# Units of 256 tokens taken in pairs of 512 from the seventh on, with g kept in the place of w_in, and a new order of the attention work

## The chip, the cores and the metric

One core of a Trainium2 chip. The metric is the device time of one execution in microseconds; the kernel before took 1070.82 us (median of 3 runs, 1069.51 to 1071.07).

## What is computed

Attention by random features over 8 batches, 8 heads, 576 tokens and head size 64, and then a feed-forward block on the 4608 tokens:

```python
h = proj - sq ; h = h - max(h) ; phi = exp(h) / sqrt(m)      # for q and k, m = 128 features
kv = einsum('bhsm,bhsd->bhmd', k_p, v) ; z = sum(k_p, axis=2)
x = einsum('bhsm,bhmd->bhsd', q_p, kv) / (einsum('bhsm,bhm->bhs', q_p, z) + 1e-06)
h = x @ w_in          # [4608, 512] @ [512, 2048]
g = h - tanh(h)
out = g @ w_out       # [4608, 2048] @ [2048, 512]
```

All matmul operands of the feed-forward block are kept as a high and a low part in the type fp32r, and each product is three matmuls: high by high, high by low, low by high.

## The kernel before

The tokens are cut into 18 units of 256 (`TC`). The weights are decoded once into 16 tiles `wt[f]` of 128 partitions, each with two parts (high, low) of 1024 columns: 512 of w_in (four blocks of 128, index `c`) and 512 of w_out. They stay in SBUF.

**First units.** Units 0 and 1 go together: `ffn_h(0, s)` has matmuls of 512 columns (12 for one of the 16 slices `f`), and four output tiles of 128 tokens are kept in four PSUM banks. This pass runs beside the decoding and the first attention work, up to about 187 us.

**Units 2 to 17.** For each unit there are 8 steps. In a step `ffn_h` (line 468) makes two slices of h with 12 matmuls of 256 columns each, into one PSUM bank (two banks, `h0` and `h1`, in turn). ScalarE takes the tanh (472), VectorE subtracts (473), ScalarE casts to the high part `gh` (474), VectorE makes the low part `gl` (475). The products with w_out for the step before, `ffn_out` (lines 486 to 488), are 12 matmuls of 512 columns into the two output banks `po0` and `po1`. So TensorE's order is h of step s, products of step s-1, h of step s+1. `ffn_store` copies the two output tiles by ScalarE (499) into one buffer of tag `o` and stores them (501).

**Attention.** `k_unit` makes for a batch `b` and a pair of heads `c` what the keys contribute, `q_unit` makes a quarter `c` of the x of a unit `ch`. There are four of each: four query quarters per unit, four key quarters per batch of 576 tokens. They are generators, run beside the feed-forward work: each call of `beat()` moves every open generator to its next `yield` and opens those that the table `start` has for this beat. A step has two beats, so a unit has 16; beat 32 is the start of unit 2 and beat 96 that of unit 6. A query quarter has 7 beats: the load (81), the high and low part of q (75, 129, 130), the features (142 to 150) and the normalisation (347 to 356), two beats of nothing, the transposes (363) with their high and low part (386, 387), the products with the keys' result (393, 394), and `x_split` (406, 407), which writes the high and low part of x into one of the two halves of `xh` and `xl`, one for even and one for odd units. If a unit is reached with `xdone[ch]` under 4, the open generators are run on until it is 4.

**Order and queues.** The instructions are put into each engine's queue by a scheduler that follows the order in which the program names them, and takes an instruction earlier where it is ready earlier. Each engine works its queue in order. All loads and stores are issued by SP's queue.

Of the kernel before, what the change touches and what calls it, by code (L numbers as in the profile page):

```python
# [19 lines left out]
P = 128  # L20
# [3 lines left out]
TC = 256  # L24
NCH = NT // TC
E = D + 2
# [5 lines left out]
def favor_attention_ffn(ctx: ExitStack, tc: tile.TileContext, qT, kT, va, vt, omT, w, out):  # L32
# [283 lines left out]
    def q_unit(ch, c):  # L316
# [47 lines left out]
        if native:  # L364
            qf = att("qt", [P, 2, TC], F32, f"qt_{n}")
            nc.scalar.copy(qf.rearrange("p h t -> p (h t)"), pt)
            yield
            pn = ps.tile([P, TC], F32, tag=bank("pt"), name=f"pn_{n}")
            for b, s, e in pieces:
                for h in range(2):  # L370
                    nc.tensor.matmul(pn[:, s:e], kvf[b][c][:, h], qf[:, h, s:e], start=h == 0, stop=h == 1)
            if ch == 2:
                if c < 2:
                    x2[c] = sb.tile([P, TC], F32, tag="xs", name=f"x2_{c}", bufs=2)
                elif c == 2:
                    x2[3] = sb.tile([P, DM], F32, tag="o", name="x2")
                    x2[2], x2[3] = x2[3][:, 0:TC], x2[3][:, TC:]
                nc.scalar.copy(x2[c], pn)
# [18 lines left out]
        nc.scalar.copy(tmp[0:D], pn[D:P, 0])  # L397
        nc.scalar.copy(tmp[D:P], pn[0:D, 1])
        nc.vector.tensor_add(xs[0:D], pn[0:D, 0], tmp[0:D])
        nc.vector.tensor_add(xs[D:P], pn[D:P, 1], tmp[D:P])  # L400
        yield
        x_split(ch, c, xs, nc.vector)
        xdone[ch] = xdone.get(ch, 0) + 1

    def x_split(ch, c, x, engine):
        nc.scalar.copy(xh[:, ch % 2, c], x)
        engine.tensor_sub(xl[:, ch % 2, c], x, xh[:, ch % 2, c].bitcast(F32))  # L407

# [47 lines left out]
    xh, xl = [sb.tile([P, 2, NC, TC], F32R, name=f"x{k}") for k in "hl"]  # L456

    def ffn_h(ch, s):

# [32 lines left out]
    def ffn_store(ch):  # L492
        for t, p in enumerate(pos[ch]):
            if ch == NCH - 1 and t == 1:
                o = sb.tile([P, DM], F32, tag="g", name=f"o_{ch}_{t}")
                nc.vector.tensor_copy(o, p)
            else:
                o = sb.tile([P, DM], F32, tag="o", name=f"o_{ch}_{t}")
                nc.scalar.copy(o, p)
            r = ch * TC + t * P  # L500
            nc.sync.dma_start(out[r : r + P, :], o)

# [5 lines left out]
    xdone = {}  # L508
    x2 = {}
    gens = []  # L510

    def tick(new=(), force=False):
# [39 lines left out]
    while decoded < NF:  # L552
# [34 lines left out]
    start = {}  # L587
    for ch in range(3, NCH):
# [8 lines left out]
    assert min(start) >= t  # L597

    def beat():
        nonlocal t  # L600
        tick(start.pop(t, ()))
        t += 1
# [3 lines left out]
    for c in range(NC):  # L606
        x_split(2, c, x2[c], nc.vector)
    ffn_out(*prev)
    ffn_store(0)
    mode.update(pj=["pj0", "pj1"], pt=["pt"])  # L610
    prev = None
    for ch in range(2, NCH):
        out_tiles(ch)
        for s in range(NS):
            while ch > 2 and xdone.get(ch, 0) < NC:
                tick((), True)
            g = (ch, s, *ffn_h(ch, s))
            beat()
            if prev is not None:
                ffn_out(*prev)  # L620
                if s == 0:
                    ffn_store(ch - 1)
            beat()
            prev = g
    ffn_out(*prev)
    ffn_store(NCH - 1)
    for name in list(pools)[::-1]:
# [36 lines left out]
```

## Time and profile before

| what | before |
|---|---|
| runs, median (lowest, highest) | 1070.82 us (1069.51, 1071.07) |
| the profiled execution, its own time | 1070.01 us |
| its span, first to last instruction | 1068.2 us |
| mean granted clock of TensorE | 0.991 |
| TensorE, VectorE, ScalarE, GpSimd busy | 1044.0, 854.0, 713.2, 323.5 us |

Times in rows count from the first instruction. In a row of groups the name of the line is followed by engine, operation, what is written and read, and the shape; x is the count, then come the busy time in us, the mean duration of one in ns, and the idle time ahead of it with what ended it. PE is TensorE's matmul, PEld its load of weights, DVE is VectorE, ACT ScalarE, POOL GpSimd, SP the engine that issues the transfers. A matmul's duration holds its way through the array, so matmuls that follow one another overlap in their rows; what a matmul costs in a full stretch is read from start to start. PEclk is the granted clock as a share of 2.4 GHz.

### The profile page before, as it was taken

How to read it: one execution, taken by the hardware profiler on the slowest of the kernel's cores; microseconds unless marked ns; L12 is line 12 of the kernel's file. 1: busy time of each engine (PE TensorE's matmuls, PEld its weight loads, DVE VectorE, ACT ScalarE, POOL GpSimd, SP SyncE). 2: the span in 40 equal slices, each digit the busy share in tenths (PEclk: the TensorE clock that was granted, in tenths of full speed). 3: DMA queues.
4: the chain of work that ended last, by engine and by line, in shares of the span. 5: the costliest groups of instructions: out<-in, count | busy, mean ns of one | idle time of the engine just before them, and what ended most of it. 6: DMA issues, size and time to landing. Idle time of an engine off the chain costs nothing. (4 is left out here: it accounts for less than half of the span.)

```text
span 1068.2 us, 20318 instructions
## 1 busy us (share of the span) xinstructions
PE 1044.0 (98%) x6760; PEld 949.3 (89%) x6760; DVE 854.0 (80%) x3030; ACT 713.2 (67%) x1833; POOL 323.5 (30%) x553
## 2 busy tenths in 40 slices
PE   8988999989999999999999999999999999999998
PEld 7767888988999999999999998999999999999997
DVE  6999985898888986788888888898888897666522
ACT  6997655777676765577777766777767775555422
POOL 4634540344333320133333333233333331000000
PEclk8999999998999999999999999999999999999999
DMA  8750401111111110011111111111101110000000
GB/s 266 234 212 12 178 4 48 43 43 38 33 53 33 53 33 31 11 53 33 52 34 52 34 28 53 33 48 29 51 22 52 29 41 11 30 11 26 1 21 20
DMA packets 35529, 55.91 MB, mean 52 GB/s; under 512 B 12256, under 2 KB 21600, under 8 KB 33376
## 3 DMA queue, kind: packets, MB, share of 16 engines
q1 hardware_dynamic: 35344, 54.57, 16.2%
q8 instruction: 54, 0.88, 0.4%
q14 instruction: 51, 0.42, 0.1%
q10 hardware_dynamic: 80, 0.03, 0.0%
HBM read 45.15 MB, written 9.44 MB: 51 GB/s over the span
## 5 line engine op out<-in xcount | busy, mean ns | idle before, releaser
L468 PE MATMUL h<-xh,w 128*128 128x256 f32 (+1 forms) x2176 | 453.3, 292 | 3.8 <-DVE g L473 2.1
L468 PEld LDWEIGHTS h<-xh,w 128*128 128x128 f32 x2176 | 356.7, 191 | 14.1 <-DVE g L473 2.7
L468 PE MATMUL h<-xl,w 128*128 128x256 f32 (+1 forms) x1088 | 317.3, 292 | 0.5 <-DVE xl L407 0.5
L486 PE MATMUL po<-w,gh 128*128 128x512 f32 x544 | 214.2, 394 | 0.0
L468 PEld LDWEIGHTS h<-xl,w 128*128 128x128 f32 x1088 | 207.9, 191 | 6.7 <-DVE xl L407 0.8
L487 PE MATMUL po<-w,gh 128*128 128x512 f32 x544 | 213.7, 393 | 0.0
L488 PE MATMUL po<-w,gl 128*128 128x512 f32 x544 | 209.3, 391 | 0.0
L473 DVE TENSOR_TENSOR g<-h,g 128x512 f32<-128x512 f32 x144 | 98.8, 686 | 66.4 <-ACT g L472 65.3
L472 ACT ACTIVATE g<-h 128x512 f32<-128x512 f32 x144 | 85.1, 591 | 99.2 <-PE h L468 91.9
L474 ACT CAST gh<-g 128x512 fp32r<-128x512 f32 x144 | 89.4, 621 | 84.3 <-DVE g L473 82.7
L475 DVE TENSOR_TENSOR gl<-g,gh 128x512 fp32r<-128x512 f32 x144 | 109.9, 764 | 38.3 <-ACT gh L474 36.5
L488 PEld LDWEIGHTS po<-w,gl 128*128 128x128 f32 x544 | 102.2, 188 | 20.7
L486 PEld LDWEIGHTS po<-w,gh 128*128 128x128 f32 x544 | 102.5, 188 | 16.6
L487 PEld LDWEIGHTS po<-w,gh 128*128 128x128 f32 x544 | 102.5, 188 | 15.2
L347 DVE CUSTOM_DVE_ANT_0 junk<-phi_q,zb 128x128 f32<-128x128 f32 (+1 forms) x320 | 96.5, 303 | 14.7 <-ACT phi_q L150 0.5
L250 POOL TENSOR_TENSOR khl<-phi_ka,khl 128x256 fp32r<-128x256 f32 x48 | 38.0, 795 | 154.2 <-DVE khl L249 129.2
L150 ACT ACTIVATE phi_q<-phi_q,nb_q 128x128 f32<-128x128 f32 x240 | 79.0, 392 | 6.3 <-DVE nb_q L146 6.1
L258 POOL CAST vhl<-v 128x128 fp32r<-128x128 f32 (+1 forms) x144 | 45.7, 319 | 100.9 <-PE pk L266 82.4
L439 POOL TENSOR_SCALAR a<-a 128x1024 f32<-128x1024 f32 x14 | 59.0, 4214 | 54.7 <-ACT a L435 42.1
L387 DVE TENSOR_TENSOR ql<-pt,qh 128x512 fp32r<-128x512 f32 x60 | 41.1, 685 | 26.5 <-ACT qh L386 26.1
L259 DVE TENSOR_TENSOR vhl<-v,vhl 128x128 fp32r<-128x128 f32 (+1 forms) x144 | 45.2, 314 | 16.7 <-POOL vhl L258 13.0
L146 DVE CUSTOM_DVE_ANT_0 phi_q<-pj_q,phi_q 128x128 f32<-128x128 f32 x240 | 55.9, 283 | 1.1 <-ACT phi_q L143 1.0
(151 smaller groups left out, 1952.9 us busy)
## 6 DMA issues: line engine op xcount, KB each, us to landing
raw<-w SPq DMA_DIRECT2D x16, 1024.0 KB, 7.5
kf<-kT SPq DMA_DIRECT2D x32, 288.0 KB, 2.9
qf<-qT SPq DMA_DIRECT2D x72, 128.0 KB, 2.1
out<-o SPq DMA_DIRECT2D x36, 256.0 KB, 2.0
v<-vt SPq DMA_DIRECT2D x24, 288.0 KB, 2.8
v<-va SPq DMA_DIRECT2D x8, 288.0 KB, 5.8
omf<-omT ACTq DMA_DIRECT2D x1, 32.0 KB, 2.1
omf<-omT SPq DMA_DIRECT2D x1, 32.0 KB, 2.4
```

Source lines behind the costliest of these rows:

```text
L146: nc.vector.tensor_tensor_reduce(ph[:, j], pj[:, i, :M], ph[:, j], scale=-SCALE, scalar=3.0e38, op0=ALU.add, op1=ALU.min, accum_out=nb[:, ...
L150: nc.scalar.activation(ph[:, j], ph[:, j], AF.Exp, bias=nb[:, j : j + 1], scale=-1.0)
L347: nc.vector.tensor_tensor_reduce(bank("junk")[r], ph[r, i], kvs[b, c][1][r, h], scale=1.0, scalar=EPS, op0=ALU.mult, op1=ALU.add, accum_ou ...
L439: engine.tensor_scalar(a.bitcast(F32), a.bitcast(F32), 2.0**-15, 122879.9921875, op0=ALU.max, op1=ALU.min)
L468: nc.tensor.matmul(o, w_, x, start=i == 0, stop=i == len(prods) - 1)
L472: nc.scalar.activation(g, p, AF.Tanh)
L473: nc.vector.tensor_sub(g, p, g)
L474: nc.scalar.copy(gh, g)
L475: nc.vector.tensor_sub(gl, g, gh.bitcast(F32))
L486: nc.tensor.matmul(po[t], h, wt[f][:, 0, DM:], start=first, stop=False)
L487: nc.tensor.matmul(po[t], h, wt[f][:, 1, DM:], start=False, stop=False)
L488: nc.tensor.matmul(po[t], l, wt[f][:, 0, DM:], start=False, stop=last)
```

## The change

From unit 6 on the units go in 6 pairs (`NL`) of 512 tokens. A pass over a pair has 16 steps, one per slice `f`. `wide_h` makes h with 12 matmuls of 512 columns, and g as before, but splits it: the first 256 tokens' g goes on to high and low part by ScalarE and VectorE, and its products with w_out (6 matmuls of 512 columns) follow one step later. The other 256 tokens' g goes by GpSimd into the columns of `wt[f]` that held the first half of w_in. After the 16 steps come the two other output tiles, 48 matmuls each, from there.

The half of w_in that is written over comes from DRAM again for the next pass: in unit 2 w_in is stored to DRAM (16 transfers of 512 KB), and from the eleventh step of the first pass on the w_in of a slice six steps ahead is brought to the columns of the second half, two tiles for one slice, in four transfers of 128 KB; `w_in` names the place. This is done for passes 1 to 5.

x no longer goes from `q_unit` to `xh` and `xl`. It goes to a tile `later` with room for two units, and is split ahead of the unit or pass that uses it: for units 3 to 6 as soon as it is there, for unit 7 behind the last h of unit 5, for the later pairs between the two late output tiles, in pieces of 512 columns. A query quarter waits with its last part until the unit two before it has been split.

A pass has 40 beats: 32 in the steps and 4 in each late output tile. The table of starts is new: listed beats for units 3 to 7 and for batches 2, 3 and 4 (28, 51, 84, with 5, 7 and 9 between the quarters), after that a query quarter every five beats (4.5 for the second pair) and a key quarter every eleven. Attention for a pair is made during the pass before it. Buffers: `kvw` 6 for 7, `qf` 1 for 2, no `tmp`; output tiles take buffers of `gl`, `gh` or `g`.

```diff
+C0 = 6
+NL = (NQ - C0) // 2
+NB = 8
...
-        tmp = att("tmp", [P, TC], F32, f"tmp_{n}")
-        xs = sb.tile([P, TC], F32, tag="xs", name=f"xs_{n}", bufs=2)
...
-        yield
-        x_split(ch, c, xs, nc.vector)
+        while ch > 3 and ch - 2 not in split:
+            yield
+        xs = later[:, c, ch % 2 * TC : ch % 2 * TC + TC]
+        nc.scalar.copy(xs[0:D], pn[D:P, 0])
+        nc.scalar.copy(xs[D:P], pn[0:D, 1])
+        nc.vector.tensor_add(xs[0:D], pn[0:D, 0], xs[0:D])
+        nc.vector.tensor_add(xs[D:P], pn[D:P, 1], xs[D:P])
         xdone[ch] = xdone.get(ch, 0) + 1
...
+    def store(p, r, engine=nc.scalar):
+        o = sb.tile([P, DM], F32, tag=bank("o"), name=f"o_{r}", bufs=1 if mode["o"][-1] == "g" else 2)
+        copy(engine, o, p)
+        nc.sync.dma_start(out[r : r + P, :], o)
+    def w_in_away(f):
+        w_dram[f] = tc.dram_tile([P, 2, DM], F32, name=f"w_in{f}")
+        nc.sync.dma_start(w_dram[f], wt[f][:, :, 0:DM].bitcast(F32))
+    def w_in_back(i):
+        f, k = i % NF, 2 * (i % NB)
+        for j in range(2):
+            for a in range(2):
+                nc.sync.dma_start(wt[k + j][:, a, TC:DM].bitcast(F32), w_dram[f][:, a, TC * j : TC * j + TC])
+    def w_in(a, f, i, c):
+        if a == 0:
+            return wt[f][:, i, c * P : (c + 1) * P]
+        j = TC + c % 2 * P
+        return wt[2 * (f % NB) + c // 2][:, i, j : j + P]
+    def wide_h(a, f):
+        p = ps.tile([P, 2, TC], F32, tag=bank("h"), name=f"h_w{a}_{f}")
+        prods = [(w_in(a, f, i, c), x[:, 0:2, c]) for c in range(NC)
+                 for i, x in ((0, xh), (0, xl), (1, xh))]
+        for i, (w_, x) in enumerate(prods):
+            nc.tensor.matmul(p, w_, x, start=i == 0, stop=i == len(prods) - 1)
+        g = sb.tile([P, 2, TC], F32, tag=bank("o"), name=f"g_w{a}_{f}", bufs=1 if mode["o"][-1] == "g" else 2)
+        e = sb.tile([P, 2, TC], F32R, tag="gh", name=f"ge_w{a}_{f}", bufs=2)
+        nc.scalar.activation(g, p, AF.Tanh)
+        nc.vector.tensor_sub(g, p, g)
+        nc.scalar.copy(e[:, 0], g[:, 0])
+        nc.vector.tensor_sub(e[:, 1], g[:, 0], e[:, 0].bitcast(F32))
+        hi, lo = [wt[f][:, i, 0:TC] for i in range(2)]
+        nc.gpsimd.tensor_copy(hi, g[:, 1])
+        nc.gpsimd.tensor_sub(lo, g[:, 1], hi.bitcast(F32))
+        return a, f, e[:, 0], e[:, 1]
...
-        phi=(ak, 3), qh=(ak, 1), ql=(ak, 1), tmp=(ak, 1), kf=(ak, 1), kx=(ak, 1), qf=(ak, 2),
+        phi=(ak, 3), qh=(ak, 1), ql=(ak, 1), kf=(ak, 1), kx=(ak, 1), qf=(ak, 1),
...
+    def begins(a):
+        return 16 * C0 + 40 * a
+    for ch in range(3, NQ):
+        a, j = (ch - C0) // 2, (ch - C0) % 2 * NC
         for c in range(NC):
-            k = 28 + 4 * c if ch == 3 else 42 + 4 * c if ch == 4 else 16 * (ch - 1) - 6 + 4 * c
+            if ch < C0 + 2:
+                k = [(28,31,34,37),(43,46,49,52),(40,55,58,64),(61,70,76,82),(67,73,79,85)][ch - 3][c]
+            else:
+                k = begins(a - 1) + (-4 + 9 * (j + c) // 2 if a == 1 else -9 + 5 * (j + c))
             start.setdefault(k, []).append(("q", ch, c))
     for b in range(2, B):
+        a = ((b * S) // TC - C0) // 2
         for c in range(NC):
-            k = 31 + 5 * c if b == 2 else 16 * (need[b] - 1) - 25 + 8 * c
+            k = [28,51,84][b - 2] + [5,7,9][b - 2] * c if b < 2 + len([28,51,84]) else begins(a - 1) + -18 + 11 * c
...
+    for a in range(NL):
+        r = (C0 + 2 * a) * TC
+        out_tiles("w")
+        prev = None
+        for f in range(NF):
+            g = wide_h(a, f)
+            beat()
+            if prev is not None:
+                wide_out(*prev)
+            i = NF * a + f + 6
+            if NF <= i < NF * NL:
+                w_in_back(i)
+            beat()
+            prev = g
+        wide_out(*prev)
+        for i in range(2):
+            store(pos["w"][i], r + i * P)
+        for i in range(2):
+            p = ps.tile([P, DM], F32, tag=bank("h"), name=f"last_{a}_{i}")
+            for f in range(NF):
+                products(p, f, *[wt[f][:, j, i * P : (i + 1) * P] for j in range(2)])
+                if f % 4 == 3:
+                    beat()
+            store(p, r + (2 + i) * P, nc.vector if a == NL - 1 and i == 1 else nc.scalar)
+            if i == 0 and a < NL - 1:
+                next_x(a + 1)
```

`products` are the three matmuls of lines 486 to 488, `wide_out` calls it for the two tiles of the first 256 tokens, and `next_x(a)` runs the attention on until the pair's x is there and then splits it.

## Rows read from the trace of the kernel before

**Rows 1.** The page: the span, busy times of the engines, and GB/s by slice.

```profile
span 1068.2 us, 20318 instructions
...
PE 1044.0 (98%) x6760; PEld 949.3 (89%) x6760; DVE 854.0 (80%) x3030; ACT 713.2 (67%) x1833; POOL 323.5 (30%) x553
...
GB/s 266 234 212 12 178 4 48 43 43 38 33 53 33 53 33 31 11 53 33 52 34 52 34 28 53 33 48 29 51 22 52 29 41 11 30 11 26 1 21 20
```

**Rows 2.** Busy time by stretch: length, engines in order, PEclk, DMA share, GB/s.

```profile
187.00:241.00 54.00, 50.72 (x340) 46.30 (x338) 47.55 (x188) 39.38 (x110) 22.88 (x46) 1.00 0.15 42
241.00:309.00 68.00, 66.21 (x435) 61.04 (x436) 61.38 (x237) 49.72 (x135) 27.35 (x54) 0.93 0.16 45
309.00:421.00 112.00, 112.00 (x769) 103.96 (x768) 92.95 (x364) 76.05 (x204) 31.07 (x60) 1.00 0.12 36
529.00:644.00 115.00, 115.00 (x793) 107.00 (x792) 98.98 (x393) 82.56 (x224) 41.42 (x80) 1.00 0.14 41
926.00:975.00 49.00, 49.00 (x326) 44.99 (x325) 31.57 (x115) 28.20 (x70) 0.00 (x0) 1.00 0.06 20
```

**Rows 3.** The same view, around the start of unit 3.

```profile
220.00:236.00 16.00, 16.00 (x105) 14.51 (x104) 15.49 (x63) 11.88 (x34) 7.95 (x16) 1.00 0.16 46
236.00:246.00 10.00, 5.19 (x25) 3.87 (x23) 8.62 (x33) 7.91 (x24) 3.75 (x12) 0.74 0.19 67
241.00:251.00 10.00, 8.21 (x34) 7.31 (x35) 9.67 (x34) 7.48 (x21) 5.26 (x11) 0.50 0.30 87
```

**Rows 4.** Timeline, TensorE's longest wait after 187 us: start, duration, instruction, idle before.

```profile
239.54 0.50 PE L142 MATMUL pj_kb<-om,kx 128*128 128x256 f32 x2 [2.82 <-DVE nb_km L146]
```

**Rows 5.** The chain that ended last, two steps of unit 17: start, duration, piece.

```profile
1044.92 2.87 PE h L468 x24
...
1050.54 2.87 PE h L468 x24
```

**Rows 6.** Timeline of TensorE, first matmul of two steps of units 0 and 1.

```profile
111.79 0.39 PE L468 MATMUL h<-xh,w 128*128 128x512 f32 x1
...
117.23 0.39 PE L468 MATMUL h<-xh,w 128*128 128x512 f32 x1
```

**Rows 7.** Groups of instructions by line and shape.

```profile
L475 DVE TENSOR_TENSOR gl<-g,gh 128x512 fp32r<-128x512 f32 x144 | 109.9, 764 | 38.3 <-ACT gh L474 36.5
...
L473 DVE TENSOR_TENSOR g<-h,g 128x512 f32<-128x512 f32 x144 | 98.8, 686 | 66.4 <-ACT g L472 65.3
L474 ACT CAST gh<-g 128x512 fp32r<-128x512 f32 x144 | 89.4, 621 | 84.3 <-DVE g L473 82.7
...
L387 DVE TENSOR_TENSOR ql<-pt,qh 128x512 fp32r<-128x512 f32 x60 | 41.1, 685 | 26.5 <-ACT qh L386 26.1
...
L250 POOL TENSOR_TENSOR khl<-phi_ka,khl 128x256 fp32r<-128x256 f32 x48 | 38.0, 795 | 154.2 <-DVE khl L249 129.2 <-PE pj_km L142 13.6 <-PE h L468 7.4
...
L407 DVE TENSOR_TENSOR xl<-xs,xh 128x256 fp32r<-128x256 f32 x60 | 27.1, 452 | 1.9 <-ACT xh L406 1.3
...
L406 ACT CAST xh<-xs 128x256 fp32r<-128x256 f32 x60 | 24.5, 409 | 20.5 <-DVE xs L400 20.2
```

**Rows 8.** Timeline of one loaded step: last h, its g, first products.

```profile
601.05 0.28 PE L468 MATMUL h<-xh,w 128*128 128x256 f32 x1
...
605.08 0.68 DVE L473 TENSOR_TENSOR g<-h,g 128x512 f32<-128x512 f32 x1
...
606.45 0.69 DVE L475 TENSOR_TENSOR gl<-g,gh 128x512 fp32r<-128x512 f32 x1 [0.69 <-ACT gh L474]
...
608.16 0.39 PE L486 MATMUL po<-w,gh 128*128 128x512 f32 x1
```

**Rows 9.** Line 475 by itself: duration min/median/max in ns.

```profile
L475 DVE TENSOR_TENSOR gl<-g,gh x144: 676/693/1525, 92.4 to 1061.1; 128x512 fp32r<-128x512 f32 x144
```

**Rows 10.** Transfers by line: count, KB each, median us from issue to landing.

```profile
qf<-qT SPq DMA_DIRECT2D x72, 128.0 KB, 2.1
```

More of the change, by code (lines that the diff above doesn't have):

```diff
@@ L24 @@
 TC = 256
-NCH = NT // TC
+NQ = NT // TC
+C0 = 6
+NL = (NQ - C0) // 2
+NB = 8
 E = D + 2
@@ L372, in q_unit @@
             if ch == 2:
[L373 to L378, printed above, removed]
+                nc.scalar.copy(later[:, c, 0:TC], pn)
             else:
@@ L394, in q_unit @@
                 nc.tensor.matmul(pn[:, h, s:e], w, ql[:, h, s:e], start=False, stop=True)
-        tmp = att("tmp", [P, TC], F32, f"tmp_{n}")
-        xs = sb.tile([P, TC], F32, tag="xs", name=f"xs_{n}", bufs=2)
[L397 to L400, printed above, removed]
-        yield
-        x_split(ch, c, xs, nc.vector)
+        while ch > 3 and ch - 2 not in split:
[5 more added lines that the diff above has]
+        nc.vector.tensor_add(xs[D:P], pn[D:P, 1], xs[D:P])
         xdone[ch] = xdone.get(ch, 0) + 1
     def x_split(ch, c, x, engine):
-        nc.scalar.copy(xh[:, ch % 2, c], x)
-        engine.tensor_sub(xl[:, ch % 2, c], x, xh[:, ch % 2, c].bitcast(F32))
+        r = ch if isinstance(ch, slice) else ch % 2
+        nc.scalar.copy(xh[:, r, c], x)
+        engine.tensor_sub(xl[:, r, c], x, xh[:, r, c].bitcast(F32))
     wt = {}
@@ L456, in favor_attention_ffn @@
     xh, xl = [sb.tile([P, 2, NC, TC], F32R, name=f"x{k}") for k in "hl"]
+    later = sb.tile([P, NC, 2 * TC], F32, name="later")
     def ffn_h(ch, s):
@@ L493, in ffn_store @@
         for t, p in enumerate(pos[ch]):
[L494 to L501, printed above, removed]
+            store(p, ch * TC + t * P)
+    def store(p, r, engine=nc.scalar):
+        o = sb.tile([P, DM], F32, tag=bank("o"), name=f"o_{r}", bufs=1 if mode["o"][-1] == "g" else 2)
+        copy(engine, o, p)
+        nc.sync.dma_start(out[r : r + P, :], o)
@@ L503, in out_tiles, with products, wide_out @@
+    def products(o, f, h, l):
+        nc.tensor.matmul(o, h, wt[f][:, 0, DM:], start=f == 0, stop=False)
+        nc.tensor.matmul(o, h, wt[f][:, 1, DM:], start=False, stop=False)
+        nc.tensor.matmul(o, l, wt[f][:, 0, DM:], start=False, stop=f == NF - 1)
+    def wide_out(a, f, h, l):
+        for t, p in enumerate(pos["w"]):
+            products(p, f, h[:, t * P : (t + 1) * P], l[:, t * P : (t + 1) * P])
     def out_tiles(ch, tags=("po0", "po1")):
@@ L508, in favor_attention_ffn @@
     xdone = {}
-    x2 = {}
+    split = {2}
     gens = []
@@ L606, in favor_attention_ffn @@
     for c in range(NC):
-        x_split(2, c, x2[c], nc.vector)
+        x_split(2, c, later[:, c, 0:TC], nc.vector)
     ffn_out(*prev)
@@ L611, in favor_attention_ffn, with x_of @@
     prev = None
-    for ch in range(2, NCH):
+    def x_of(ch):
+        split.add(ch)
+        for c in range(NC):
+            x_split(ch, c, later[:, c, ch % 2 * TC : ch % 2 * TC + TC], nc.vector)
+    for ch in range(2, C0):
         out_tiles(ch)
+        while xdone[ch] < NC:
+            tick((), True)
+        if ch not in split:
+            x_of(ch)
         for s in range(NS):
-            while ch > 2 and xdone.get(ch, 0) < NC:
-                tick((), True)
+            if s > 0 and ch + 1 not in split and xdone.get(ch + 1) == NC:
+                x_of(ch + 1)
             g = (ch, s, *ffn_h(ch, s))
+            if ch == C0 - 1 and s == NS - 1 and xdone.get(C0 + 1) == NC:
+                x_of(C0 + 1)
             beat()
@@ L622, in favor_attention_ffn @@
                     ffn_store(ch - 1)
+            if ch == 2:
+                for f in range(2 * s, 2 * s + 2):
+                    w_in_away(f)
             beat()
@@ L625, in favor_attention_ffn, with next_x @@
     ffn_out(*prev)
-    ffn_store(NCH - 1)
+    ffn_store(C0 - 1)
+    mode.update(o=["g", "gl"])
+    def next_x(a):
+        pair = (C0 + 2 * a, C0 + 2 * a + 1)
+        for ch in pair:
+            while xdone.get(ch, 0) < NC:
+                tick((), True)
+        if split.isdisjoint(pair):
+            for c in range(NC):
+                x_split(slice(0, 2), c, later[:, c].rearrange("p (j t) -> p j t", j=2), nc.vector)
+            split.update(pair)
+        for ch in pair:
+            if ch not in split:
+                x_of(ch)
+    next_x(0)
+    for a in range(NL):
[24 more added lines that the diff above has]
+                next_x(a + 1)
     for name in list(pools)[::-1]:
```

8 lines of the change are left out of this document (4 added, 4 removed).

## The prediction

> **What bounds the kernel now.** I read the page first [rows 1]: TensorE is busy for 1044.0 of 1068.2 us, VectorE for 854.0. "Busy" is modelled for matmuls, so the stage table comes next [rows 2]: from 309 us on TensorE has no idle time, also where VectorE stands at 0.86 (98.98 of 115.00 us in 529 to 644). The time is therefore the sum of matmul start-to-start intervals, and an edit off TensorE matters only where it makes TensorE wait. From 187 us on it idles 3.28 + 1.79 us, nearly all of it in one stop: 4.81 us between 236 and 246 us, where unit 2 ends and unit 3 needs its x [rows 3]. The longest wait in it is 2.82 us for VectorE [rows 4], which had been at 15.49 of 16.00 us just before. Right behind the stop the granted clock is 0.50 for 10 us: the 1.2 GHz level, so about 5.0 us more are lost. That place costs 4.8 + 5.0 = 9.8 us.
>
> **The first products, 512 columns for 256.** A step now has 24 matmuls of 256 columns and 12 of 512; near the end, without attention, steps start 5.62 us apart (1044.92 to 1050.54), 2.87 of it for the 24 [rows 5]. The pass over units 0 and 1 already has the new shape, 12 and 12 of 512 columns: 5.44 us (111.79 to 117.23) [rows 6]. Both stretches ran at 2.4 GHz. Same columns, 0.18 us less a step; the change has 6 pairs of 16 steps, so 96 x 0.18 = 17.3 us, all on the path. Bounds: reading either interval 0.02 off gives 15 to 19. The two late output tiles of a pair need the same 96 matmuls of 512 columns that the steps had, so they cost nothing in sum; they only move to the end of the pass.
>
> The rows show 2 x 119.6 ns for two matmuls of 256 columns and 226.7 for one of 512, 12.5 ns between them. The Trainium skill, TensorE: Matmul & The Clock Gate, section "Back-to-back issue gap", speaks against the change: its isolated gap is columns/2.4 + 2.5 ns, so joining two matmuls would save one fixed 2.5 ns; as an estimate from that page, 1152 pairs give 2.9 us for 17.3.
>
> **The attention order.** By the start of unit 6 (beat 96) the old table has started the query work of units 3 to 6 and two quarters of 7, and the keys of batches 2 and 3. The new one has all of unit 7, just begun unit 8, and the first keys of batch 4 done and the second begun: some 3 query and 1.2 key quarters more. Prices: unit 926 to 975 has 8 steps and four query quarters; VectorE's 31.57 less 8 x 1.45 (two operations of 0.686 and 0.764) leaves 5.0 us each, TensorE's 49.0 less 8 x 5.62 leaves 1.0 each [rows 2, 7]. Two units 529 to 644 have eight query and four key quarters: VectorE 98.98 - 23.2 - 40 = 35.8, 8.9 a key quarter; TensorE 115 - 89.9 - 8 = 17, 4.3 each. So 25.7 us of VectorE and 8.2 of TensorE move ahead of unit 6 and leave the later part: no gain or loss in the sum by itself. For 187 to 421 us that means VectorE 201.9 + 25.7 = 227.6 against TensorE 234 - 5.1 idle - 5.0 clock + 8.2 = 232: VectorE at 0.98. Unit 3's query quarters start up to three beats earlier and its x is split as soon as it is there, not at the last beat, so the stop at 236 should go (-9.8). What is late next is g: VectorE's work queues ahead of it. Lower bound 0, as TensorE was full for 16 us with VectorE at 0.97; upper bound, VectorE never fuller than the 0.903 of 241 to 309, 227.6/0.903 = 252, 20 us over 232. I take +6, nearer to the 0.97, because late attention may run on into the first pass.
>
> **The passes.** In a loaded step now, h ends at 601.33 (601.05 + 0.28), its g at 607.14, and the products that need it start at 608.16 [rows 8]: 6.83 us to use, 5.81 used. Of the 6.83, 2.87 + 2.75 are the step's own matmuls and 1.2 attention. Afterwards the cover is 12 + 6 matmuls of 0.227 us and the same 1.2, 5.3 us; the chain loses 0.21 on ScalarE (621 to 409 ns) and 0.31 on VectorE (764 to 452) [rows 7], 5.3 us: no slack at such a step. TensorE can take the next h first, as the second bank comes free before the casts. Bounds: 0, and 0.5 us at each of the 64 steps of the four heaviest passes, 32. I take 5, a microsecond a pass for five passes, at their start, where only h covers the chain; the sixth has no attention.
>
> GpSimd gets 192 instructions of 128x256, at most 0.795 us each [rows 7], 153 us, beside the path; its results are wanted at the pass's end. VectorE's 0.764 has a median of 0.693 and a maximum of 1.525 [rows 9], while the same size with one operand in PSUM takes 0.685 [rows 7]: meeting GpSimd costs it up to a whole GpSimd instruction. The 5.0 us a pair that VectorE is spared (16 x 0.31) go into more such meetings. The Trainium skill, SBUF — State Buffer, section "Who interferes with whom", has that rule: a VectorE instruction with two SBUF inputs and a GpSimd one that reads SBUF hold each other up for a whole instruction; the trace agrees.
>
> **What I cost at nothing.** w_in goes out in unit 2 (16 x 512 KB), and comes back in passes 0 to 4, 512 KB a step in four transfers, like the query loads in size (2.1 us to landing) [rows 10]. 512 KB in 5.3 us is 99 GB/s, 140 with the 41 of [rows 2]; the start of the kernel moved 266 [rows 1]. They go six steps ahead of use. SP is passed by 336 more issues; a load that waits for its buffer holds them up, and with one query buffer for two loads go out one quarter earlier, some 13 us, for two. Cover gone, the first products wait. Stores share buffers with g: 3 us held against a step of 5.6. The last tile's copy and store stay as they are.
>
> **Sum.** The profiled execution took 1070.0 (span 1068.2 and 1.8 around it), 0.8 below the median of the runs. 1070.0 - 17.3 - 9.8 + 6 + 5 = 1053.9; against the median 1054.7, so 1055.
>
> **Rivals.** (1) VectorE becomes the bound before unit 6 and eats the gain: the upper bound, +20 for +6, gives 1069, half of it 1062. For: 0.98 asked for. Against: what is ahead of time can wait. 1062 to 1072, 0.16. (2) Slower: the first products of a pass wait for x. Place: the pass starts, as x is taken over only 48 matmuls (10.9 us) before its use, after attention that ends some three beats earlier. Price: each such stop 9.8 us, idle and half clock, as at 236. From the second on, 1055 + 19.6 = 1074.6, it is slower; four give 1094. For: it happened so at unit 3. Against: 10.9 us cover a chain of some 4 (a cast of 0.62, four subtractions of up to 0.764). 0.13. (3) The fixed cost per matmul is less than the rows say: with a sixth of it the sum is 1055 + 14.4 = 1069, no change. The 2.9 us of the page cited above would be this case. Against: two stretches of rows. 0.05. (4) w_in doesn't return in time: at 100 GB/s with all else stopped a step is 5.2 us for 4.1, over 80 steps +93, 1148. Against: [rows 1]. 0.03. My forecast, 1043 to 1062: 0.63.
>
> **Numbers.** A measurement of this kernel tells 0.2% from no change, 2.1 us: 1068.7 to 1072.9 is the same. Faster: 0.63, 0.11 of rival 1, 0.02 of 3: 0.76. Same: 0.05 + 0.03 + 0.01 = 0.09. Slower: 0.12 of rival 2 and rival 4: 0.15. Range: 1043 (the sum with no new stalls, 17.3 + 9.8 off) to 1075 (rival 2 at two stops); some 0.17 lies outside.
>
> **What would show it.** Right: steps of 4.1 us and attention in the passes, 96 matmuls of 512 columns without a gap at their end, no clock of 0.50 after 187 us, TensorE idle for under 12 us from there, VectorE above 0.95 in units 2 to 5. Wrong: first products 0.24 us apart; TensorE waiting on VectorE's g; half clock at the pass starts; waits on a DMA.

## The result, and the profile after

1074.87 us (median of 6 runs, 1074.26 to 1076.31) against 1070.94 for the kernel before, measured beside it: ratio 1.0039, interval 1.0029 to 1.005. The change is slower by 3.9 us; the forecast was 1055. The profiled execution's span is 1072.4 us.

The page, to be set beside [rows 1]:

```profile
span 1072.4 us, 19097 instructions
PE 1039.7 (97%) x5608; PEld 887.8 (83%) x5608; DVE 857.9 (80%) x3010; ACT 694.4 (65%) x1813; POOL 440.2 (41%) x745
```

TensorE has 1152 matmuls less and hardly less busy time. By the durations of [rows 7] the shorter instruction should have relieved VectorE of 96 x 0.31 = 30 us, and it is busier by 3.9: its instructions got longer.

Busy time by stretch, columns as in [rows 2]; from 421 us on the stretches are passes:

```profile
187.00:241.00 54.00, 52.96 (x356) 48.22 (x355) 48.26 (x190) 40.02 (x112) 23.09 (x44) 1.00 0.12 33
241.00:309.00 68.00, 65.84 (x457) 60.58 (x457) 63.82 (x259) 53.00 (x144) 27.00 (x48) 1.00 0.16 47
309.00:421.00 112.00, 109.84 (x722) 98.89 (x721) 104.33 (x409) 83.22 (x224) 39.04 (x73) 1.00 0.13 37
421.00:441.00 20.00, 16.64 (x86) 14.28 (x85) 17.36 (x72) 16.00 (x46) 10.02 (x22) 0.83 0.28 95
431.00:438.50 7.50, 6.03 (x24) 5.27 (x24) 6.49 (x24) 6.00 (x18) 4.61 (x11) 0.54 0.13 42
529.00:644.00 115.00, 112.89 (x588) 95.10 (x586) 103.71 (x388) 80.07 (x220) 59.35 (x112) 1.00 0.38 115
873.00:975.00 102.00, 102.00 (x497) 85.68 (x496) 58.73 (x212) 50.01 (x127) 20.15 (x32) 1.00 0.33 102
```

Three things to see. Up to 421 us the stop ahead of unit 3 is gone and the clock stays at 1.00, but TensorE idles 1.04 + 2.16 + 2.16 = 5.4 us, as much as before (3.28 + 1.79), with VectorE at 0.89, 0.94 and 0.93. At the start of the first pass it idles 3.4 us, and the clock falls to 0.54 for 7.5 us. In the second pass, where the kernel before had no idle time, it idles 2.1 us beside a GpSimd at 0.52; the late pass 873 to 975 has none. Only the larger gaps show as idle, since a matmul's duration covers its successor's start. Read from the start of each matmul to the start of the next, with 0.120 and 0.227 us taken off for every matmul of 256 and 512 columns and some 0.116 for the narrower ones, 187 to 421 us holds 10.2 us of waiting (before 9.1), 421 to 441 6.9, and 441 to 975 11.6 (before 0).

The chain that ended last, two steps of the last pass, which has no attention beside it:

```profile
1002.84 2.72 PE h_w L529 x12
1006.92 2.72 PE h_w L529 x12
```

A step is 4.08 us; with the 6 late matmuls of 0.227 (1.36 us) 5.44, the value read from [rows 6]: 0.18 less than [rows 5].

TensorE's waits from 187 us on (total, times, longest), the first of them:

```profile
PE h_w L529 <- DVE g_w L533: 2.7, 4, 1.3
PE pk L269 <- POOL khl L253: 1.9, 3, 1.5
PE pk L305 <- DVE c L302: 1.3, 2, 1.0
PE pt L366 <- DVE phi_q L359: 1.3, 2, 1.0
PE h L468 <- DVE g L473: 1.3, 1, 1.3
PE po_w L544 <- DVE ge_w L535: 1.2, 3, 0.8
```

Those of the whole list are short and add up to 13.1 us, 10.9 of them on VectorE; none is on a transfer. TensorE's timeline at the first pass's start:

```profile
417.60 0.39 PE L529 MATMUL h_w<-xh,w 128*128 128x512 f32 x1
...
426.06 0.39 PE L529 MATMUL h_w<-xh,w 128*128 128x512 f32 x1
...
432.74 0.77 PE L269 MATMUL pk<-khl,vhl 128*128 128x256 f32 x2 [1.47 <-POOL khl L253]
...
434.59 1.05 PE L529 MATMUL h_w<-xh,w 128*128 128x512 f32 x2
...
439.09 0.39 PE L529 MATMUL h_w<-xh,w 128*128 128x512 f32 x1
```

The pass begins at 417.60. By 426.06 the h of its first two slices has 18 of its 24 matmuls; the last 6, from 434.59 on, need the fourth quarter of x. Between them there is only attention, which waits on VectorE and GpSimd. The two slices after them, from 439.09 on, come behind the g of the first two, and so 4.5 us later. The last three quarters of x for this pass reach `later` 10.0 and 9.3 us apart, the last of them 15 us after the pass has begun:

```profile
412.95 0.43 DVE L399 TENSOR_TENSOR later<-pn,later 64x256 f32<-64x256 f32 x1
422.99 0.43 DVE L399 TENSOR_TENSOR later<-pn,later 64x256 f32<-64x256 f32 x1
432.25 0.43 DVE L399 TENSOR_TENSOR later<-pn,later 64x256 f32<-64x256 f32 x1
```

Groups of instructions, and the durations of two lines (min/median/max, ns):

```profile
L350 DVE CUSTOM_DVE_ANT_0 junk<-phi_q,zb 128x128 f32<-128x128 f32 x256 | 83.6, 328 | 12.6 <-ACT phi_q L153 1.0 <-DVE dn L350 1.0
L538 POOL TENSOR_TENSOR w<-g_w,w 128x256 fp32r<-128x256 f32 x96 | 79.5, 828 | 5.1
L535 DVE TENSOR_TENSOR ge_w<-g_w,ge_w 128x256 fp32r<-128x256 f32 x96 | 51.3, 535 | 15.4 <-ACT ge_w L534 14.7
L537 POOL CAST w<-g_w 128x256 fp32r<-128x256 f32 x96 | 39.7, 415 | 221.6 <-DVE g_w L533 209.5
...
L535 DVE TENSOR_TENSOR ge_w<-g_w,ge_w x96: 390/426/1003, 444.6 to 1045.9; 128x256 fp32r<-128x256 f32 x96
L533 DVE TENSOR_TENSOR g_w<-h_w,g_w x96: 654/687/693, 437.9 to 1044.8; 128x512 f32<-128x512 f32 x96
```

The half-size subtraction takes 0.535 us, not the 0.452 of [rows 7], with single ones at 1.0. Line 533, which reads one of its operands from PSUM, never takes more than 0.693 us.

### The profile page after: what moved, and what is told of

It reads as the page before. It is cut to its first block, busy times and chain, and to the rows that moved or that the text cites. A ratio compares the mean times of both kernels' runs of the same rounds, so it can differ in the third digit from the quotient of the medians.

```text
span 1072.4 us, 19097 instructions
## 1 busy us (share of the span) xinstructions
PE 1039.7 (97%) x5608; PEld 887.8 (83%) x5608; DVE 857.9 (80%) x3010; ACT 694.4 (65%) x1813; POOL 440.2 (41%) x745
## 4 chain that ended last, share of the span: by engine, by line
PE 55%; DVE 30%; ACT 7%; issue 5%; DMA 1%; POOL 1%; SPq 0%; DVEq 0%; POOLq 0%; ACTq 0%
PE h_w L529 15%; PE h L468 7%; DVE junk L350 4%; PE last L543 3%; PE last L544 3%; PE last L542 3%; PE po_w L544 3%; PE po_w L542 2%; PE po_w L543 2%; DVE phi_q L359 2%; PE po L486 2%; PE po L487 2%; PE po L488 2%; DVE g_w L533 2%; DVE vhl L262 2%
## 5 line engine op out<-in xcount | busy, mean ns | idle before, releaser
L529 PE MATMUL h_w<-xh,w 128*128 128x512 f32 x768 | 254.0, 394 | 2.7 <-DVE g_w L533 2.7
L529 PEld LDWEIGHTS h_w<-xh,w 128*128 128x128 f32 x768 | 143.8, 189 | 30.9 <-DVE g_w L533 4.4
L468 PE MATMUL h<-xh,w 128*128 128x256 f32 (+1 forms) x640 | 146.8, 307 | 5.0 <-DVE g L473 3.3
L529 PE MATMUL h_w<-xl,w 128*128 128x512 f32 x384 | 150.7, 393 | 0.0
L468 PEld LDWEIGHTS h<-xh,w 128*128 128x128 f32 x640 | 107.4, 190 | 12.5 <-DVE g L473 4.1
L468 PE MATMUL h<-xl,w 128*128 128x256 f32 (+1 forms) x320 | 98.0, 307 | 0.3 <-DVE xl L405 0.3
L529 PEld LDWEIGHTS h_w<-xl,w 128*128 128x128 f32 x384 | 72.5, 189 | 12.8
L538 POOL TENSOR_TENSOR w<-g_w,w 128x256 fp32r<-128x256 f32 x96 | 79.5, 828 | 5.1
L542 PE MATMUL po_w<-w,ge_w 128*128 128x512 f32 x192 | 75.8, 395 | 0.3 <-ACT ge_w L534 0.3
L544 PE MATMUL last<-w 128*128 128x512 f32 x192 | 75.3, 392 | 0.0
L543 PE MATMUL last<-w 128*128 128x512 f32 x192 | 75.3, 392 | 0.0
L542 PE MATMUL last<-w 128*128 128x512 f32 x192 | 75.2, 392 | 0.0
L543 PE MATMUL po_w<-w,ge_w 128*128 128x512 f32 x192 | 75.2, 392 | 0.0
L544 PE MATMUL po_w<-w,ge_w 128*128 128x512 f32 x192 | 70.7, 396 | 1.2 <-DVE ge_w L535 1.2
```

The source lines that it names most:

```text
L468: nc.tensor.matmul(o, w_, x, start=i == 0, stop=i == len(prods) - 1)
L529: nc.tensor.matmul(p, w_, x, start=i == 0, stop=i == len(prods) - 1)
L538: nc.gpsimd.tensor_sub(lo, g[:, 1], hi.bitcast(F32))
L542: nc.tensor.matmul(o, h, wt[f][:, 0, DM:], start=f == 0, stop=False)
L543: nc.tensor.matmul(o, h, wt[f][:, 1, DM:], start=False, stop=False)
L544: nc.tensor.matmul(o, l, wt[f][:, 0, DM:], start=False, stop=f == NF - 1)
```

## The experiments

**GpSimd's share left out.** The three lines that write the late 256 tokens' g into the weight tiles are taken out; the late output tiles then multiply what w_in left in these columns.

```diff
-        hi, lo = [wt[f][:, i, 0:TC] for i in range(2)]
-        nc.gpsimd.tensor_copy(hi, g[:, 1])
-        nc.gpsimd.tensor_sub(lo, g[:, 1], hi.bitcast(F32))
```

> The changed kernel took 1074.9 us. This one leaves out the two GpSimd instructions of each of the 96 steps of the passes (the late output tiles are then multiplied from what w_in left in their place, the same matmuls). Theory A: GpSimd's 192 instructions lengthen VectorE's instructions (its busy time is 857.9 us although 33 us of work were taken off it), and the full VectorE makes TensorE wait about 11 us in the steps of passes 0 to 2. Then VectorE's busy time falls by 25 to 35 us and the time to 1062 to 1068. Theory B: the new attention order is what costs, as it fills VectorE ahead of unit 6; then the waits before unit 6 and at the start of the first pass stay, and the time is 1070 to 1074. Theory C: the transfers of w_in cost; then 1075.

1065.76 us, 9.1 less than the change (ratio to before 0.9955, 0.9944 to 0.9967). Its page and the same two stretches:

```profile
PE 1036.3 (97%) x5608; PEld 889.5 (84%) x5608; DVE 835.3 (79%) x3010; ACT 697.0 (66%) x1813; POOL 321.3 (30%) x553
...
421.00:441.00 20.00, 16.63 (x86) 14.29 (x85) 17.60 (x70) 14.68 (x43) 9.29 (x20) 0.83 0.29 92
...
529.00:644.00 115.00, 114.91 (x606) 97.71 (x606) 101.84 (x414) 82.33 (x227) 40.06 (x81) 1.00 0.39 116
```

VectorE's busy time falls by 22.6 us although none of its instructions was taken out, and the idle time inside the pass goes (2.1 to 0.1 us). The start of the first pass is unchanged. So the time is theory A's, with a fall of VectorE's busy time a little below its 25 to 35 us, and the waits ahead of unit 6 and at the pass's start, which theory B names, stay as well.

**The late cast on ScalarE**, only the subtraction left on GpSimd (`nc.scalar.copy(hi, g[:, 1])`).

> The changed kernel with the late half's cast on ScalarE (96 x 0.41 us) and only its subtraction on GpSimd (96 x 0.83). If each microsecond of GpSimd costs alike (40 of 119 us leave): a third of the 9.1 us that the run without GpSimd gave, 1071 to 1073. If only the subtraction, which reads two tensors, gets in VectorE's way: 1074 to 1076. If ScalarE's added 39 us delay the tanh: over 1076.

1074.27 us (1.0029, 1.0018 to 1.004): 0.6 us less, no difference that these intervals tell. VectorE's busy time falls from 857.9 to 852.6 us, ScalarE's rises from 694.4 to 723.4. Moving the cast gains nothing here; whether it costs nothing on GpSimd, or ScalarE's added work takes the gain away, this run does not tell.

**The same work put into the kernel before**, with its result not read: first both instructions, then the subtraction alone, in each of the 96 steps from unit 6 on.

```diff
+        if ch >= 6:
+            for i in range(2):
+                gx = sb.tile([P, TC], F32R, tag="gx", name=f"gx{i}_{ch}_{s}")
+                if i == 0:
+                    nc.gpsimd.tensor_copy(gx, gh[:, 1].bitcast(F32))
+                else:
+                    nc.gpsimd.tensor_sub(gx, gh[:, 1].bitcast(F32), gl[:, 1].bitcast(F32))
         return gh, gl
```

> The kernel before, with the change's GpSimd work added and nothing else: from unit 6 on each of the 96 steps has a GpSimd cast and a GpSimd subtraction of 128x256, whose result nobody reads. Before took 1070.9 with VectorE busy for 854.0. Theory A: VectorE's busy time rises by 20 to 35 us and TensorE waits; as a narrow step has 6.8 us to make g where a wide one has 5.3, somewhat less than the 9.1 us found: 1073 to 1080. Rival (it costs only together with the wide steps): VectorE's busy time rises, the time stays 1070 to 1072.

1090.36 us (1.0179, 1.0165 to 1.0193): 19.3 us, above both ranges and twice the 9.1 us that the same work costs in the change.

> The kernel before, with one GpSimd instruction of 128x256 added to each of the 96 steps from unit 6 on: the subtraction with two operands in SBUF (its result is not read); the cast that stood beside it in the run with both is left out. Both together took 1090.4 us, 19.3 more than the kernel before. Theory, that VectorE is held up by GpSimd's subtraction and hardly by its cast: 1084 to 1090 us, and VectorE's 128x512 subtraction of line 475 nearly as long as with both. Rival, that any GpSimd instruction counts by its busy time: the subtraction has some two thirds of it, 1081 to 1084. Rival, that the two cost alike: 1079 to 1081.

1088.97 us (1.0173, 1.0159 to 1.0187): the subtraction costs as much alone. Rows of this run, the last one of 529 to 644 us:

```profile
PE 1056.2 (97%) x6760; PEld 951.3 (87%) x6760; DVE 877.0 (81%) x3030; ACT 712.2 (66%) x1833; POOL 391.9 (36%) x649
...
L347 DVE CUSTOM_DVE_ANT_0 junk<-phi_q,zb 128x128 f32<-128x128 f32 x256 | 86.8, 340 | 13.1 <-ACT phi_q L150 0.5
...
529.00:644.00 115.00, 112.34 (x753) 102.11 (x752) 101.83 (x382) 79.80 (x215) 49.65 (x93) 1.00 0.13 40
```

and line 347 of the kernel before, which is not among the rows ahead of the prediction:

```profile
L347 DVE CUSTOM_DVE_ANT_0 junk<-phi_q,zb 128x128 f32<-128x128 f32 x256 | 76.5, 301 | 12.4 <-ACT phi_q L150 0.5 <-ACT tmp L398 0.5
```

Nobody reads what these subtractions make; they hold 68 us of GpSimd's time (391.9 less 323.5) and lengthen VectorE's by 23.0, 10.3 of it in this one group, which reads two operands from SBUF. TensorE idles 2.7 us in a stretch that had none [rows 2]. But VectorE is not the only way by which they cost. They read `gh`, and from 421 us on ScalarE's cast into its next buffer waits for GpSimd, as it never did in the kernel before:

```profile
ACT gh L474 <- POOL khl L250: 12.4, 7, 2.9
```

TensorE, too, waits there 2.5 us in 9 places for GpSimd's part of the keys, and in the kernel before for none of it. In the change the cast of line 534 never waits for GpSimd, and the wait for the keys is as long with GpSimd's share as without it (1.9 and 2.1 us). So the 9.1 us of the first experiment are the price of the share in the change; of the 18 to 19 us here, what goes by VectorE and what by GpSimd's queue was not taken apart.

**The transfers of w_in left out** (neither stored nor brought back; the later passes multiply what lies in the columns).

> The changed kernel without the transfers of w_in, out in unit 2 and back in the passes (the later passes then multiply x by what lies in the second half's place, the same matmuls). Theory C: TensorE or the loads of q and k wait for the 50 MB: 1055 to 1066. Theories A and B: no trace of a wait for them on TensorE, 1073 to 1076.

1075.37 us (1.0044, 1.0032 to 1.0056), the change's own time within these intervals. No cost of the transfers shows.

**The new order without pairs** (`C0 = 18`, so all units narrow and w_in left where it is; the new starts for units 3 to 7 and batches 2 to 4, the old formula behind them), and **the same with the old starts throughout**, which leaves of the change the tile `later`, the split of x as soon as it is there, and the buffers. The second kernel against the first:

```diff
-                k = [(28,31,34,37),(43,46,49,52),(40,55,58,64),(61,70,76,82),(67,73,79,85)][ch - 3][c]
+                k = 28 + 4 * c if ch == 3 else 16 * (ch - 1) - 6 + 4 * c
...
-            k = [28,51,84][b - 2] + [5,7,9][b - 2] * c if b < 2 + len([28,51,84]) else 16 * (need[b] - 1) - 25 + 8 * c
+            k = 31 + 5 * c if b == 2 else 16 * (need[b] - 1) - 25 + 8 * c
```

> The new attention order without the pairs: all units from 2 on stay at 256 tokens, x goes by the later tile, the starts of units 3 to 7 and batches 2 to 4 are the new ones, those behind have the old formula; no transfers of w_in. Before took 1070.9. Theory A (GpSimd in the passes): the order costs little, 1066 to 1073, the stop at the start of unit 3 (9.8 us) is gone or spread. Theory B (the order): TensorE waits 10 us in units 2 to 5 and 5 to 10 more around the start of unit 6, without the 15 us that the wide matmuls save: 1078 to 1085. Theory C: 1061 to 1066, as nothing but the stop changes.

> The change without pairs and with the old table of starts: what is left is that x goes by the later tile and is split as soon as it is there. The same kernel with the new starts took 1072.1, before 1070.9. Theory: the tile takes away the stop at unit 3 (9.1 us of waiting between 187 and 425 us in before), and the denser starts alone put 10 us of waiting back. Then 1061 to 1065 here. Rival: the new, earlier starts took the stop away, and the tile costs nothing and gives nothing: 1070 to 1073.

New starts: 1072.13 us (1.0012, 1.0004 to 1.0021). Old starts: 1062.46 us (0.993, 0.9916 to 0.9943), the fastest of all. The stretches with new starts:

```profile
241.00:309.00 68.00, 65.97 (x459) 60.68 (x458) 64.02 (x256) 53.16 (x145) 27.01 (x48) 1.00 0.16 47
309.00:421.00 112.00, 109.97 (x736) 99.51 (x735) 104.33 (x414) 84.10 (x227) 38.92 (x73) 1.00 0.12 37
```

and with old ones:

```profile
236.00:246.00 10.00, 10.00 (x84) 9.80 (x83) 9.53 (x39) 8.71 (x23) 5.83 (x13) 1.00 0.22 59
241.00:309.00 68.00, 67.82 (x468) 62.51 (x467) 61.75 (x240) 50.67 (x139) 28.70 (x56) 1.00 0.18 53
309.00:421.00 112.00, 111.58 (x758) 102.98 (x757) 92.24 (x354) 74.86 (x197) 27.69 (x52) 1.00 0.12 36
```

The stop of [rows 3] goes by the tile and the earlier split (10.00 of 10.00 us, clock 1.00), without any new start. The new starts then ask VectorE for 0.93 to 0.94 instead of 0.82 to 0.91, TensorE idles 4.1 us in place of 0.6 in these two rows, and the whole costs 1072.13 - 1062.46 = 9.7 us.

**VectorE relieved of normalisation** in the change (`norm` half on ScalarE, for a quarter of it).

> The changed kernel with half instead of a quarter of the normalisations on ScalarE (60 instructions of 0.334 us leave VectorE, 20 us; ScalarE gets 25 us). Theories A and B both say that a full VectorE is what TensorE waits for, so they expect 1060 to 1069, and VectorE at 0.90 or less where it was 0.93 (309 to 421 us). Theory C (transfers): 1074 to 1076. If ScalarE, at 0.74 to 0.78 there, is as much in the way: over 1076.

1076.62 us (1.0053, 1.0037 to 1.0069; single runs from 1073.17 to 1078.32): what theories A and B expected is missed, and the median lies just above 1076, where ScalarE was expected to be as much in the way. VectorE's busy time falls by 11.7 us to 846.2, but in 241 to 309 us TensorE waits more:

```profile
241.00:309.00 68.00, 63.59 (x423) 57.84 (x423) 62.28 (x242) 52.94 (x147) 25.74 (x49) 0.97 0.16 46
```

VectorE stays at 0.92 and ScalarE at 0.78. At the start of the first pass it is the other way: TensorE idles 2.0 us in 421 to 441, in place of 3.4, at a clock of 0.93. So that VectorE's load as such is what TensorE waits for in units 2 to 5 is not shown; the order of work may be as much of it.

**Pairs only where they come late.** From unit 12 on (three pairs; units 9 to 13's starts at some 0.8 of the old distance), then one pair (units 16, 17) and two (14 to 17) with the old starts kept up to the last eight or sixteen quarters, which are hurried to end ahead of the pass.

```diff
-C0 = 6
+C0 = 16
...
-                k = [(28,31,34,37),(43,46,49,52),(40,55,58,64),(61,70,76,82),(67,73,79,85)][ch - 3][c]
+                k = [(28,32,36,40),...,(233,236,239,242),(244,246,247,248)][ch - 3][c]
```

> The change with its pairs only from unit 12 on (3 passes in place of 6), and the starts of before for units 3 to 7; units 8 to 13 and their keys get some 0.8 of the old spacing, so that x of unit 13 is there when the first pass begins. Theory A (the wide matmuls pay, but GpSimd's share lengthens VectorE's instructions where VectorE is nearly full): the passes now lie where VectorE has room, so nearly all of 3 x 2.5 to 2.9 us is kept and the wait in the passes is under 2 us; with before's stop at unit 3 back: 1062 to 1067. Rival (the denser attention ahead of the first pass costs what the passes save, as in the change): 1068 to 1073.

> The kernel of the run with the old starts, with units 16 and 17 as one pair. Its pass has no attention beside it and VectorE is at a quarter there, so GpSimd's share costs nothing and the wide matmuls give 2.5 to 2.9 us: 1058 to 1063. Ahead of it only the eight last query quarters start earlier (233 to 248 for 234 to 262), where VectorE was at 0.64. Rival: that density brings a wait or a stop at the pass's start, and the saving is lost: 1063 to 1069.

> The same with two pairs, units 14 to 17; the last keys start five beats apart (193 to 208) and 12 query quarters three beats apart ahead of unit 14. If only a density that keeps VectorE above 0.93 over several units costs: 5.0 to 5.8 us saved, a few lost, 1057 to 1063. If any attention pulled ahead of a pass costs as in the run with pairs from unit 12 (23 us for three pairs): 1065 to 1076.

1080.14 us (1.0087, 1.0073 to 1.0101), 1070.29 us (1.0003, 0.9994 to 1.0012) and 1080.23 us (1.0096, 1.0082 to 1.011): all missed. With pairs from unit 12, the units with denser starts and the pass's start:

```profile
530.00:640.00 110.00, 107.71 (x715) 96.26 (x714) 104.05 (x404) 81.65 (x224) 44.66 (x85) 1.00 0.14 41
640.00:770.00 130.00, 125.92 (x833) 113.24 (x832) 118.83 (x475) 96.09 (x266) 50.61 (x94) 1.00 0.13 38
770.00:800.00 30.00, 24.60 (x124) 20.08 (x123) 29.06 (x103) 23.33 (x61) 15.82 (x30) 0.94 0.30 89
```

With VectorE at 0.91 to 0.95 TensorE idles 6.4 us in 240, without any GpSimd instruction of a pair. At the start of the pass it idles 5.4 us. What these pairs cost is read against the kernel with the old starts and no pair (1062.46 us): one pair costs 7.8 us, two 17.8, three 17.7.

**The pass's start.** One pair again, units 16 and 17 started at 228 to 236 and 238 to 244 in place of 233 to 242 and 244 to 248.

> The kernel with one pair (units 16 and 17), with its last eight query quarters started earlier: unit 16 at beats 228 to 236 for 233 to 242, unit 17 at 238 to 244 for 244 to 248, with batch 7's keys and unit 15's quarters drawn forward by two to five beats to make room. With one pair the first products of the pass met three unfinished query quarters, one after the other 4.6 us apart, and TensorE idled 6.6 us and then ran at half clock. Theory that the stop at a pass's start is only a matter of when the last quarters end: the stop goes, 1059 to 1062 us. Rival, that the denser quarters before it cost as much (units 11 to 13 lost some 6 us when two pairs asked for such a density): 1064 to 1068. Rival, that the place of x is the cause (the second unit's half comes free only with the last h of the unit before): the stop stays, 1068 to 1071.

1070.46 us (1.0001, 0.9992 to 1.001): the stop stays, as the second rival had it. TensorE's timeline, taken in the fastest of the 11 runs (1067.83 us), shows why it need not be the rival's reason:

```profile
945.77 0.60 PE L366 MATMUL pt<-ident,phi_q 128*128 128x128 f32 x4
...
956.46 0.60 PE L366 MATMUL pt<-ident,phi_q 128*128 128x128 f32 x4
...
965.74 0.60 PE L366 MATMUL pt<-ident,phi_q 128*128 128x128 f32 x4
...
972.75 0.63 PE L366 MATMUL pt<-ident,phi_q 128*128 128x128 f32 x4 [1.82 <-DVE later L399]
...
977.73 0.74 PE L529 MATMUL h_w<-xh,w 128*128 128x512 f32 x2 [2.16 <-ACT xh L404]
```

Started two beats apart (one step, 5.6 us or a little more), the last quarters come out 7 to 11 us apart, each behind the one before. In the code a quarter's transposes and its products use the same PSUM bank, and the one at 972.75 waits for the predecessor's last addition into `later`; that this bank sets the pace of all of them is read from the code and this one wait. So the lead was made even: all starts behind beat 74 drawn together, the last at 240, 246 or 250; then two pairs in the same way.

> One pair (units 16 and 17), with all starts behind beat 74 drawn together evenly: a query quarter every 3.5 beats for 4, the last one at beat 240 for 248, the keys with them. In the run before, the last four quarters, started two beats apart, came out 7 to 11 us apart all the same, so they can't be hurried at the end. Theory that a quarter's way through its one PSUM bank sets this pace and that only an even lead brings the second unit's x in time: TensorE's idle time at the pass's start falls from 5 us to under 2, and since VectorE asks for some 0.91 to 0.93 in the units before it, 1060 to 1065 us. Rival that the second unit's x can't come before the last h of the unit ahead whatever the starts: 5 us of idle stay, 1069 to 1072. Rival that even this density costs TensorE 5 us or more in units 6 to 15: 1066 to 1070 with no stop at the pass.

> The same with a quarter every 3.66 beats and the last one at beat 246. By the theory of the pace, the last quarters are again unfinished when the pass starts, but fewer: 1 to 3 us idle there, 1062 to 1067 us. By the rival of the place of x the stop is as long as with the last quarter at 240.

> One pair with an even lead and the last quarter at beat 250 (a quarter every 3.74 beats). With the last at 246 there was no stop and 1063.9 us, with 240 likewise and 1066.4, and the difference lay in the units before, where the denser table has more waits. Theory, that only density counts as long as the last quarter ends in time: if 250 is still in time, 1060 to 1063 us; if the last quarter is late there, one stop of 2 to 5 us, 1064 to 1067.

> Two pairs (units 14 to 17) with an even lead: all starts behind beat 74 drawn together to a quarter every 3.64 beats, the last one ahead of the passes at beat 216. With the last sixteen quarters hurried it took 1080.2 us, with 15 us lost at the pass's start and 6 in the units before. Theory of the pace: no stop at the start of the first pass; each pair saves 2.9 us (16 steps by 0.18), the units before lose 3 to 5: 1060 to 1066 us, and GpSimd's share costs little, since little attention runs beside these passes. Rival, that a pass with attention beside it loses what it saves: 1066 to 1071.

In order: 1066.39 us (0.9956, 0.9943 to 0.9968), 1063.91 us (0.9936, 0.9922 to 0.9949), 1065.78 us (0.9958, 0.9944 to 0.9971), and two pairs 1065.65 us (0.9952, 0.994 to 0.9965). The pass's start with the last quarter at 246:

```profile
960.00:982.00 22.00, 22.00 (x112) 18.76 (x111) 8.84 (x16) 8.53 (x18) 3.01 (x6) 1.00 0.07 25
```

and at 250:

```profile
956.00:985.00 29.00, 26.52 (x132) 21.83 (x131) 12.44 (x39) 11.66 (x28) 3.59 (x6) 1.00 0.05 19
```

At 246 the stop is gone, where 1 to 3 us were expected; at 250 2.5 us of it are back; and at 240, also without a stop, the units before pay instead, as the second rival of that run had it, if for less (in 756 to 873 us TensorE idles 1.26 us, with the last at 246 0.29). With two pairs 1.5 us of idle time are left in 868 to 880 us, around the start of the first pass (granted clock 0.93), where none was expected. So the place of x was not the cause, as it is the same in all of these; how evenly and how late the quarters are started is. But no kernel with a pair is faster than the one without pairs (1062.46): even with the stop gone, one pair (1063.91) gains nothing over it. The kernel with the last quarter at 240 has one more thing to show:

```profile
529.00:644.00 115.00, 114.71 (x790) 105.75 (x788) 107.03 (x431) 86.99 (x240) 44.14 (x89) 1.00 0.14 41
```

VectorE is at 0.93 and TensorE idles 0.3 us; with the change's starts, also at 0.93, it idled 2.0 in 309 to 421. So VectorE's share alone does not set the price; in this stretch a table with equal distances is cheaper at the same share. Which quarter meets which in the change's table was not taken apart.

## Why the prediction was wrong

The parts, each from its own kernel or rows, so that they need not add up: the tile and the earlier split of x -8.0 us (1062.46 less 1070.41); the denser starts +9.7; the start of the first pass +6.9; GpSimd's share +9.1; the transfers 0; the wide matmuls -17.3 by the step. That gives +0.4; measured +3.9, so 3.5 us are not assigned. Waits in the passes beyond GpSimd's share, 11.6 less 9.1, would be 2.5 of them.

- **The first products** (-17.3): right. The step came out as 4.08 + 1.36 us where TensorE is full. The Trainium skill, TensorE: Matmul & The Clock Gate, section "Back-to-back issue gap", would, as an estimate from its formula, have given 2.9 us; the trace does not bear that out.
- **The stop ahead of unit 3 gone** (-9.8): right in place; of its two reasons the tile with the earlier split was enough, and the earlier starts were not needed. Measured -8.0 for all that came with the tile. The 9.8 counted the idle 1.79 us of 241 to 251 us also at half clock; without that the rows give 4.8 + 4.1 = 8.9.
- **VectorE full ahead of unit 6** (+6, bounds 0 and 20): this term was mis-sized. It measured 9.7. I had taken a value near the lower end, from 16 us in which TensorE was full beside VectorE at 0.97; over 234 us at 0.89 to 0.94, less than the 0.98 that I had worked out, that did not hold. Together with the stop, -3.8 was forecast and +1.7 came.
- **The passes** (+5, bounds 0 and 32): this is the step that failed most. It priced the chain h to g alone; the passes held 6.9 us of waiting at the first start and 11.6 behind it, 9.1 of them by GpSimd's share: 18.5 in all. That lies inside the bounds, but neither of the two causes was in the term's value.
- **GpSimd "beside the path"**: wrong. The meeting was named, and seen in [rows 9], and its size was not far off: 5.0 us a pair, 30 in all, were allowed for, and VectorE lost 22.6. But I set this against what VectorE was to be spared, and that was 18.7 us and not 30 (854.0 less the 835.3 of the run without GpSimd's share); and I put its price for TensorE at nothing, where it was 9.1 us, in passes with attention in which VectorE stands at 0.9.
- **Rival 2** (x late at a pass's start, 9.8 us each) happened at one pass of six, for 6.9 us. I had set 10.9 us of cover against the split of x and had not asked whether the last quarters themselves would be done. In the change the last three came 9 to 10 us apart, the last of them 15 us after the pass had begun. What makes them late there stays open: the kernel meant to tell, with batch 4's keys later, deadlocks and has no time, and an even lead was tried with one and two pairs only.
- **Rival 1** (VectorE as the bound) named the engine on which most of the waits end, but VectorE was never full: TensorE waited beside it at 0.9 to 0.94, and also in the passes, where I had not looked for it. That relieving it did not help (`norm`), and that the even table costs less beside 0.93, says that its load alone is not the cause.
- **w_in and SP's queue** at nothing: right, as far as the run without the transfers shows.

## What to carry to other kernels

Work given to an engine beside the path was not free here, because it lengthened the instructions of a nearly full engine that the path waits for. Before giving such work, put it into the old kernel with its result unread, and time that; then look in the trace for waits that the added work makes itself, since here the price in the old kernel was twice the one in the change. When work is moved ahead of its use, move it evenly over a long stretch: here the last pieces came out 7 to 11 us apart although they were started closer together, and the consumer's first matmuls met the one that was late. A change that has a gain in one part and costs in others is worth taking apart: here the smallest part, one tile with the earlier split, was worth 8 us, and the rest cost more than it saved.

## What the runs showed of the hardware

In the kernel before, 96 GpSimd subtractions of two SBUF operands lengthened VectorE's busy time by 23.0 us, 0.24 us each; with 96 casts of the same size beside them it was 877.4 us in place of 877.0. A cast is not without effect, though: in the change its move to ScalarE took 5.3 us off VectorE (857.9 to 852.6), and in the run with both instructions a subtraction of VectorE's own that takes 0.42 us alone takes 0.66 where it starts together with an added cast:

```profile
966.36 0.66 DVE L130 TENSOR_TENSOR qx<-qf,qx 64x256 fp32r<-64x256 f32 x1
...
966.34 0.40 POOL L480 CAST gx<-gh 128x256 fp32r<-128x256 f32 x1 [4.02 <-ACT gh L474]
```

So the cast costs VectorE less than the subtraction, and how much in all depends on what it meets. The Trainium skill, SBUF — State Buffer, section "Who interferes with whom", has a VectorE instruction with two SBUF inputs and a GpSimd instruction that reads SBUF hold each other up for the whole instruction. The trace agrees that VectorE is held up by both, the subtraction and the cast, and not where one of its operands is in PSUM (line 535: 0.390 us at least, 1.003 at most; line 533: 0.654 and 0.693); the 0.24 us lost beside the cast above are less than its whole 0.40.

Idle time and clock did not go together simply. With one pair and the last quarters at 238 to 244, TensorE idled 5.0 us in 960 to 982 us and the granted clock stayed at 1.00 in the profiled run, whose mean clock of 0.997 is the highest of that kernel's 11 runs; the others had 0.993 to 0.997, and took up to 1071.74 us. In the change 3.4 us of idle time in 421 to 441 us came with 0.54 for 7.5 us. What decides it is not settled by these runs.
